# Half of the layer norm with features on the partitions, in a fused attention and MLP kernel on one core

## The chip, the core and the metric

One core of a Trainium2 chip runs the program. The core has five engines with a queue each: PE (matmuls; its weight loads are listed as PEld), DVE, ACT and POOL (elementwise work), and SP, which here issues most transfers. An engine takes its instructions in the order in which the program lists them. Transfers are carried out by 16 DMA engines. The metric is the device time of one execution in microseconds (us), median over runs; less is better.

## The reference

```python
xn = (x - mean(x)) / sqrt(var(x) + 1e-5)              # x: 2048 tokens x 512 features
q, k, v = split(xn @ wqkv)                            # 32 heads of 16 features
s = softmax(q @ k.T / 4) @ v @ wo
h = relu(xn @ w1 + b1) ** 2                           # 1792 hidden features
out = x + s * silu(h @ w2 + b2)
```

Everything is float32. The kernel gets that accuracy from faster matmuls by splitting an operand into a high part (rounded) and a low part (the rest), and adding three products: high x high, high x low, low x high.

## The kernel before

The 2048 tokens are handled as 16 tiles of 128 (t = 0 to 15) and as four chunks of 512 (c = 0 to 3). All matmuls on the normalised input need it with features on the partitions: `xTs[c]` holds chunk c as [128 partitions, high/low, 4 feature blocks, 512 tokens].

**Lead-in, up to the first side round.** For each tile: `load_x` loads 128 tokens on the partitions; `ln_stats` takes mean and variance on DVE (L1369, L1371) and the root of the variance on ACT (L1373); `ln_norm` forms scale and offset on DVE (L1378, L1379) and applies them (DVE L1383 for tiles 0 and 1, ACT L1387 behind that); `ln_high` transposes the tile with four matmuls against the identity (PE L1394) and copies the high part out of PSUM (ACT L1396); `ln_low` subtracts to get the low part (DVE L1402). The weights for the first projections come as `wm` (query and key columns of the first eight heads) and `wv` (value columns), and are split by ACT and POOL (`split_w`, L1136, L1137, L116, L117).

Projections of a finished chunk are PE work in tiles of 12 matmuls, 512 columns wide: `qk_tile(m, c)` (L1207; m = 0 to 3 are queries, 4 to 7 keys, eight heads each) and `v_tile(c, tt)` for 128 tokens (L1273). For chunk 0, queries and keys go in two halves of 256 columns. A tile occupies one PSUM bank until ACT has copied it out; queries and keys are then split by POOL, or, for the quick ones, by ACT and DVE (L122, L123), and stored to the memory tensors `q_d` and `k_d` (L1162); values go through one of seven buffers `vt` to `v_d` (L1285). PE's list is mixed by the loop over i, which pumps some matmuls of the oldest open tile behind each tile's transposes.

Before the first side round PE has done 16 tiles: keys m = 4 of all four chunks, queries m = 0 of chunks 0 to 2, values of chunks 0 and 1 and the first of chunk 2. The keys of the first four heads are read back into `ka` (12 loads, L181) and the queries into `qm` (L170). Part of `xTs` is also written out for the MLP (`spill`, L1458, and two copies into a free `ka` buffer, L1538).

**Side rounds.** From L1303 on, PE does the other projections in halves of 64 partitions, two at a time, mixed with the score matmuls from which DVE takes the row maxima (L401, L408). The rest of the kernel (exponentials, products with the values, the MLP, the output projection) follows; its order comes from planned tables. The change leaves all of that as it is.

**What sets the order.** In the lead-in the orders of PE, DVE, ACT and POOL are those in which the code is written. SP's order is set by the framework's scheduler until the side rounds begin, and by the code from there on. Transfers use eight semaphores in turn, so that a transfer is issued only when the one eight places before it has landed.

Of the kernel before, what the change touches and what calls it, by code (L numbers as in the profile page):

```python
# [9 lines left out]
F32 = mybir.dt.float32  # L10
# [63 lines left out]
def kernel(  # L74
    ctx: ExitStack,
    tc: tile.TileContext,
    x: bass.AP,
    wqkv: bass.AP,
# [18 lines left out]
    sp_d = dram.tile([S, D], F32, name="sp_d")  # L97
    xn_d = dram.tile([2, P, KO, S], F32, name="xn_d")
# [33 lines left out]
    with ExitStack() as ph:  # L132
# [42 lines left out]
        def load_k(qd, n):  # L175

            p, j, i = n // 6, n // 3 % 2, n % 3
            if n % 6 == 0:
                kas[qd, p] = ring("ka")
            h = 4 * qd + 2 * p + j  # L180
            nc.sync.dma_start(  # L181
                kas[qd, p][64 * j + DH * i : 64 * j + DH * (i + 1), :].bitcast(F32),
                k_d[h // 8][i % 2, (h % 8) * DH : (h % 8 + 1) * DH, :],
            )
# [13 lines left out]

        def load_q(u, name):
            tiles = []  # L200
            for p in range(2):
                load_q_pair(u, name, p, tiles)
            return tiles
# [928 lines left out]
        def split_w(dst, kos, cols, raw, pool=False):  # L1132
            if pool:
                split((dst[:, 0, kos, cols], dst[:, 1, kos, cols]), raw)
                return
            nc.scalar.activation(dst[:, 0, kos, cols], raw, AF.Copy)  # L1136
            nc.gpsimd.tensor_tensor(  # L1137
                dst[:, 1, kos, cols], raw, dst[:, 0, kos, cols].bitcast(F32), op=ALU.subtract
            )

        def load_w(name, width, at, kos=(KO,)):
            raw = st.tile([P, KO, width], F32, name=name)
            k0 = 0
            for n in kos:
                nc.sync.dma_start(
                    raw[:, k0 : k0 + n],
                    wqkv[:, at + k0 * width : at + (k0 + n) * width].rearrange(
                        "p (k n) -> p k n", n=width
                    ),
                )  # L1150
                k0 += n
            return raw
# [28 lines left out]
        held = []  # L1181
        hold = [True]

        def when_done(fn):
            if hold[0]:
                held.append(fn)
            else:
                fn()

        def let_go():  # L1190
            while held:
                held.pop(0)()

# [8 lines left out]
        def qk_tile(m, c):  # L1202
# [750 lines left out]
```

## Time and profile before

| | |
|---|---|
| median of 3 runs | 1571.35 us (1570.82 to 1571.38) |
| profiled execution | 1571.16 us, of which the span of instructions is 1569.3 |
| transfers, 0 to 20 us | 83% of the 16 DMA engines busy, 291 GB/s |
| 20 to 40 us | 96%, 305 GB/s |
| 40 to 60 us | 91%, 218 GB/s |
| PE's first transposes | at 6.21 us |
| PE's first side round | at 62.36 us |

The views are read so. The page gives busy time and share of each engine, and the chain of work that ended last. A list of waits names, for an engine, whose end ended its idle time: total, count, longest. A timeline has start, length, engine, line, operation, operands and shape, count, and in brackets the idle time before. A row of windows has the stretch, its length, then busy time and instructions of PE, PEld, DVE, ACT and POOL, PE's granted clock, the share of the DMA engines that was busy, and GB/s. Groups (by line and shape) have count, total busy time, mean ns of one, and idle time before them.

### The profile page before, as it was taken

The page shows a single profiled execution, that of the slowest core. Times are in us where ns is not written, and L with a number is a line of the kernel's source. Part 1 is how long each engine was busy: PE and PEld are TensorE (multiplying, and loading weights), DVE is VectorE, ACT ScalarE, POOL GpSimd, SP SyncE. Part 2 cuts the span into 40 slices and gives each one's busy share as a digit, 9 for nine tenths or more (in the row PEclk, how much of TensorE's full clock was granted, in tenths as well). Part 3 has the DMA queues.
Part 4 walks back from the last instruction along what each step waited for, and adds up shares of the span by engine and source line. Part 5 has one row for each costly group of instructions (what it writes and reads, how often), then busy time and mean ns, then how long its engine had stood idle before and what let it go on. Part 6 is the DMA issues. An engine that isn't in the chain of part 4 may idle for free.

```text
span 1569.3 us, 34206 instructions
## 1 busy us (share of the span) xinstructions
PE 1557.0 (99%) x12364; PEld 872.9 (56%) x12364; DVE 1342.3 (86%) x2307; ACT 1279.3 (82%) x2507; POOL 805.9 (51%) x824
## 2 busy tenths in 40 slices
PE   8999999999999999999999999999999999999998
PEld 7899755555555555555555555555555555555553
DVE  7377899999989998999899999998999999887765
ACT  7222788888889888888898888888888888888886
POOL 6346787348645543354465434545654345654621
PEclk9999999999999999999999999999999999999999
DMA  8967666224544531345244322533552143347665
GB/s 296 255 237 233 198 200 183 51 58 129 173 111 137 148 88 38 77 142 129 73 137 139 71 56 72 157 103 81 145 150 57 37 107 90 75 119 220 205 203 179
DMA packets 152216, 210.11 MB, mean 134 GB/s; under 512 B 58192, under 2 KB 71248, under 8 KB 150480
## 3 DMA queue, kind: packets, MB, share of 16 engines
q1 hardware_dynamic: 151904, 207.67, 46.5%
q8 instruction: 98, 1.61, 0.4%
q14 instruction: 70, 0.57, 0.1%
q10 hardware_dynamic: 144, 0.26, 0.0%
HBM read 141.56 MB, written 63.68 MB: 131 GB/s over the span
## 4 chain that ended last, share of the span: by engine, by line
PE 98%; DVE 1%; DMA 1%; issue 0%; ACT 0%; SPq 0%; DVEq 0%
PE se L487 17%; PE se L1434 12%; PE po L487 9%; PE pd_t L275 8%; PE pm_t L275 8%; PE pm_t L401 7%; PE pm_t L1434 7%; PE se L401 5%; PE pm_t L487 5%; PE pm_t L1303 4%; PE po L1434 4%; PE pd_t L401 2%; PE pm_t L243 2%; PE po L401 1%; PE pd_t L1303 1%; PE se L1273 1%
## 5 line engine op out<-in xcount | busy, mean ns | idle before, releaser
L408 DVE TENSOR_REDUCE mx<-pm_t 128x1 f32<-128x512 f32 x898 | 590.2, 682 | 50.3 <-PE pm_t L401 36.7
L1446 ACT ACTIVATE pt<-se 128x512 f32<-128x512 f32 x983 | 570.5, 623 | 30.4 <-PE pm_t L275 10.2
L408 DVE TENSOR_REDUCE mx<-se 128x1 f32<-128x512 f32 x716 | 478.3, 684 | 90.5 <-PE se L401 62.5
L1434 PE MATMUL se<-qe,ka 64*128 64x512 f32 x1086 | 434.4, 414 | 0.0
L401 PE MATMUL pm_t<-ka,qm 64*128 64x512 f32 x898 | 347.8, 398 | 0.0
L1446 ACT ACTIVATE pt<-pm_t 128x512 f32<-128x512 f32 x546 | 326.9, 622 | 8.9 <-PE pm_t L275 3.9
L1434 PEld LDWEIGHTS se<-qe,ka 64*128 64x128 f32 x1086 | 195.6, 184 | 201.6 <-ACT pt L1446 129.6
L487 PE MATMUL se<-pt,v 128*32 128x512 f32 x2224 | 282.1, 602 | 0.0
L401 PE MATMUL se<-ka,qm 64*128 64x512 f32 x716 | 281.8, 412 | 0.0
L1683 POOL TENSOR_TENSOR sum<-sum,sum 128x512 f32<-128x512 f32 x99 | 127.8, 1291 | 186.3 <-ACT sum L1682 185.9
L1683 POOL TENSOR_TENSOR ot<-ot,sum 128x512 f32<-128x512 f32 x99 | 127.7, 1290 | 180.2 <-ACT sum L1682 180.0
L1434 PE MATMUL pm_t<-qe,ka 64*128 64x512 f32 x575 | 219.0, 407 | 0.0
L275 PE MATMUL pm_t<-w2t,hT 64*128 64x512 f32 x780 | 206.6, 398 | 0.0
L1446 ACT ACTIVATE pt<-po 128x512 f32<-128x512 f32 x299 | 186.7, 625 | 7.8 <-PE pm_t L275 3.8
L401 PEld LDWEIGHTS pm_t<-ka,qm 64*128 64x128 f32 x898 | 164.0, 184 | 35.6 <-DVE mx L408 4.0
L275 PE MATMUL pm_t<-xc,w1s 64*128 64x512 f32 x672 | 177.3, 396 | 0.0
L275 PE MATMUL pd_t<-xc,w1s 64*128 64x512 f32 (+1 forms) x672 | 170.9, 388 | 0.0
L408 DVE TENSOR_REDUCE mx<-pd_t 128x1 f32<-128x512 f32 x233 | 158.7, 681 | 1.5 <-PE pd_t L401 1.5
L408 DVE TENSOR_REDUCE mx<-po 128x1 f32<-128x512 f32 x201 | 137.4, 683 | 22.2 <-PE po L401 18.7
L275 PE MATMUL pd_t<-w2t,hT 64*128 64x512 f32 x564 | 149.3, 397 | 0.0
L401 PEld LDWEIGHTS se<-ka,qm 64*128 64x128 f32 x716 | 131.4, 184 | 21.0 <-DVE mx L408 7.9
L275 PEld LDWEIGHTS pm_t<-w2t,hT 64*128 64x128 f32 x780 | 139.5, 184 | 4.4
(225 smaller groups left out, 2956.9 us busy)
## 6 DMA issues: line engine op xcount, KB each, us to landing
w1s<-w_d SPq DMA_DIRECT2D x84, 256.0 KB
w2t<-w_d SPq DMA_DIRECT2D x42, 512.0 KB
qm<-q_d SPq DMA_DIRECT2D x384, 32.0 KB
ka<-k_d SPq DMA_DIRECT2D x96, 128.0 KB
qe<-q_d SPq DMA_DIRECT2D x384, 32.0 KB
q_d<-hl SPq DMA_DIRECT2D x16, 512.0 KB
g<-g_d SPq DMA_DIRECT2D x32, 256.0 KB
k_d<-hl SPq DMA_DIRECT2D x15, 512.0 KB
```

The lines of the kernel that those rows point to most:

```text
L243: mm = nc.tensor.matmul(out_() if callable(out_) else out_, lh(r), rh(r), start=first_ and lane == 0, stop=last_ and lane == 1, skip_group ...
L275: mm = nc.tensor.matmul(out_() if callable(out_) else out_, lh(r), rh(r), start=first_ and lane == 0, stop=last_ and lane == 1, skip_group ...
L401: nc.tensor.matmul(ps, qms[u][p][64 * j : 64 * j + 64, qb * P : (qb + 1) * P], kas[qd, p][64 * j : 64 * j + 64, kc * 512 : (kc + 1) * 512] ...
L408: return nc.vector.tensor_reduce(mxs[u][:, c, kc : kc + 1], ps, axis=AX.X, op=ALU.max)
L487: nc.tensor.matmul(po[32 * j : 32 * j + 32, :], vs[qd][:, (4 * kb + j) * VW : (4 * kb + j) * VW + 32], pts[j], start=first, stop=last, ski ...
L1273: nc.tensor.matmul(out_, lh(slice(0, P)), rh(slice(0, P)), start=first_, stop=last_)
L1303: mm = nc.tensor.matmul(out_, lh(r), rh(r), start=first_ and lane == first, stop=last_ and lane != first, skip_group_check=True,)
L1434: nc.tensor.matmul(se, kas[qd, j // 2][b : b + 64, kb * P : (kb + 1) * P], qes[u][j // 2][b : b + 64, :], start=True, stop=True,)
L1446: return nc.scalar.activation(pts[j], se, AF.Exp, scale=0.25)
L1683: nc.gpsimd.tensor_tensor(pos["sum"], pos["sum"], part, op=ALU.add)
```

## The change

Tiles 0 to 7 are handled as before, except that PE's transposes are a step of their own (`ln_turn`). For chunks 2 and 3 the host lays out a second input, the same x with features on the partitions: `A_x_columns`, four groups (g = 2 to 5) of 256 tokens. For each group the tokens are also loaded with tokens on the partitions, two to a partition (`load_rows`), only to take mean and variance (`row_stats`). For a chunk, the moments of its 512 tokens, [128, 2 groups, mean or 1/deviation, 2], are written to memory (`row_out`) and read back to every partition (`row_in`, 512 KB), both from ACT's queue. DVE then subtracts the mean and multiplies by 1/deviation on the columns (`column_norm`, two operations on 128 x 1024), ACT copies the high part (`column_high`), DVE forms the low part (`column_low`). There are no transposes for these eight tiles. Column group 2 is loaded into the buffer of `wm`; groups 3, 4 and 5 share two buffers.

The lead-in is a written list of steps instead of a loop, with SP's transfers in it. Three other things move in it: the value weights are split by ACT and POOL as the other weights are; the first keys are read back in pieces, chunks 0 and 1 together (12 loads of half the old size), chunk 2 alone (12 of a quarter), and chunk 3 directly from the buffer in SBUF (12 moves), some of them from ACT's queue; the spills and copies for the MLP and the two bias loads stand behind the keys.

```diff
+        def row_stats(g, j):
+            c, h = divmod(g + 2, 2)
+            if h == j == 0:
+                moments[c] = xp.tile([P, 2, 2, 2], F32, name="mvg", bufs=2)
+            stats = xp.tile([P, 6], F32, name="stats")
+            nc.vector.bn_stats(stats, rows[g][:, j])
+            nc.vector.bn_aggr(moments[c][:, h, :, j], stats)
...
+        def row_out(c):
+            nc.scalar.dma_start(st_d[c], moments[c])
+
+        def row_in(c):
+            spread[c] = xp.tile([P, P, 2, 2, 2], F32, name="sb", bufs=2)
+            nc.scalar.dma_start(
+                spread[c].rearrange("p a h s j -> p (a h s j)"),
+                st_d[c].rearrange("a h s j -> (a h s j)")[None, :].to_broadcast([P, 1024]),
+            )
+
+        def column_norm(g, i):
+            c, h = divmod(g + 2, 2)
+            v = columns[g].rearrange("p k (a j) -> p k a j", j=2)
+            nc.vector.tensor_tensor(
+                v, v, spread[c][:, None, :, h, i, :].to_broadcast([P, KO, P, 2]),
+                op=(ALU.subtract, ALU.mult)[i],
+            )
+
+        def column_high(g):
+            c, h = divmod(g + 2, 2)
+            nc.scalar.activation(
+                xTs[c][:, 0, :, h * 256 : (h + 1) * 256], columns[g], AF.Copy
+            )
+
+        def column_low(g, eng):
+            c, h = divmod(g + 2, 2)
+            sl = slice(h * 256, (h + 1) * 256)
+            eng.tensor_tensor(
+                xTs[c][:, 1, :, sl], columns[g], xTs[c][:, 0, :, sl].bitcast(F32),
+                op=ALU.subtract,
+            )
...
-        for i in range(NT + 3):
...
+        ln_scale(3)
+        ln_root(4)
+        ln_turn(2)
+        ln_norm(3)
...
+        ln_turn(3)
+        ln_stats(6)
+        ln_norm(4)
+        matmuls(("qk", 0, 0), 12)
...
+        load_columns(5)
...
+        move_k(5, nc.scalar)
+        fill_ring("qe", 0, 0.0)
+        load_k(0, 1, 2, 3, nc.sync)
+        load_k(0, 3, 2, 3, nc.scalar)
...
+        "A_x_columns": _np.asarray(inputs["A_x"])
+        .reshape(S, D)[1024:]
+        .reshape(4, 256, KO, P)
+        .transpose(0, 3, 2, 1),
```

Rows of the built programs show the three places that matter for PE. The first is the start of PE's list, before the change (`pm_t` are transposes, `se` the first projections of chunk 0, 256 columns wide, from `xT_193`):

```order
L1394 MATMUL pm_t<-ident,xn 128x128 x8
L1207 MATMUL se<-xT_193,wa_t 128x256 x10
L1394 MATMUL pm_t<-ident,xn 128x128 x4
L1207 MATMUL se<-xT_193,wa_t 128x256 x6
L1394 MATMUL pm_t<-ident,xn 128x128 x4
L1207 MATMUL se<-xT_193,wa_t 128x256 x8
L1394 MATMUL pm_t<-ident,xn 128x128 x4
```

The same place on PE after the change, where chunk 0 is `xT_195`:

```order
L1408 MATMUL pm_t<-ident,xt 128x128 x8
L1238 MATMUL se<-xT_195,wa_t 128x256 x12
L1408 MATMUL pm_t<-ident,xt 128x128 x8
L1238 MATMUL se<-xT_195,wa_t 128x256 x36
L1408 MATMUL pm_t<-ident,xt 128x128 x4
```

The transposes of tile 3 used to come behind 16 matmuls, six of them of the second projection tile, and now come behind 12, straight after those of tile 2; the other 36 matmuls of the first two projection tiles stand behind them.

The second place is the end of the normalising on DVE. Before the change (`xT_192` is chunk 3, `hl` are quick key and query splits, `mx` the first row maxima):

```order
L1402 TENSOR_TENSOR xT_192<-pm_t,xT_192 128x4x128
L1378 RECIPROCAL rstd<-rstd 128x1
L1379 TENSOR_SCALAR rstd<-mv,rstd 128x1
L1402 TENSOR_TENSOR xT_192<-pm_t,xT_192 128x4x128 x3
L123 TENSOR_TENSOR hl<-se,hl 128x512 x2
L123 TENSOR_TENSOR hl<-po,hl 128x512
L408 TENSOR_REDUCE mx<-se 128x1 x70
```

After the change (`sb` are the spread moments, `wm` and `xc` the columns, `xT_197` and `xT_194` chunks 2 and 3):

```order
L1464 TENSOR_TENSOR wm<-wm,sb 128x1024 x2
L1464 TENSOR_TENSOR xc<-xc,sb 128x1024 x2
L1478 TENSOR_TENSOR xT_197<-wm,xT_197 128x4x256
L1478 TENSOR_TENSOR xT_197<-xc,xT_197 128x4x256
L1464 TENSOR_TENSOR xc<-xc,sb 128x1024 x4
L1478 TENSOR_TENSOR xT_194<-xc,xT_194 128x4x256 x2
L1270 TENSOR_TENSOR hl<-se,hl 128x512
L405 TENSOR_REDUCE mx<-se 128x1 x70
```

The small steps per tile have become twelve wide ones in a row, and both products of the last group stand ahead of both low parts of chunk 3.

The third place is ACT around the last tiles of the list. Before the change (`vt` are copies of value tiles, `hl` of keys and queries):

```order
L122 ACTIVATE hl<-se 128x512
L1282 ACTIVATE vt_200<-se 128x32x16
L1282 ACTIVATE vt_201<-se 128x32x16
L1282 ACTIVATE vt_202<-se 128x32x16
L1282 ACTIVATE vt_196<-pd_t 128x32x16
L122 ACTIVATE hl<-po 128x512
L1282 ACTIVATE vt_197<-pd_t 128x32x16
```

After the change (`ka<-hl` are moves of chunk 3's keys, `ka<-k_d` loads of chunk 2's):

```order
L1260 ACTIVATE hl<-se 128x512
L1286 DMA ka_210<-hl 16x512 x2
L1254 ACTIVATE vt_204<-se 128x32x16
L1286 DMA ka_210<-hl 16x512
L184 DMA ka_210<-k_d_61 16x512 x3
L1286 DMA ka_211<-hl 16x512
L1254 ACTIVATE vt_198<-pd_t 128x32x16
L1286 DMA ka_211<-hl 16x512 x2
L184 DMA ka_211<-k_d_61 16x512 x2
L1264 ACTIVATE raw<-po 128x512
```

ACT now issues twelve of the key transfers, and the copies that free PSUM banks stand between them: the copy of the first tile in the bank `pd_t` comes behind three loads that need chunk 2's stored keys.

More of the change, by code (lines that the diff above doesn't have):

```diff
@@ L97 @@
     sp_d = dram.tile([S, D], F32, name="sp_d")
+    st_d = {c: dram.tile([P, 2, 2, 2], F32, name=f"st_d{c}") for c in (2, 3)}
     xn_d = dram.tile([2, P, KO, S], F32, name="xn_d")
@@ L197, in load_v @@
             vs[qd] = v
[L199 to L203, printed above, removed]
         def load_q_pair(u, name, p, tiles):
@@ L1404, in ln_low, with load_rows @@
             )
-        ahead = []
-        rest = []
-        order = []
-        def pump(n):
-            for _ in range(n):
-                while True:
-                    todo = ahead or rest
-                    if not todo:
-                        return
-                    if next(todo[0], todo) is not todo:
-                        break
-                    todo.pop(0)
+        rows, moments, columns, spread = {}, {}, {}, {}
+        def load_rows(g):
+            rows[g] = xp.tile([P, 2, D], F32, name="xg", bufs=3)
+            nc.sync.dma_start(
+                rows[g], xf[512 + g * 256 : 768 + g * 256, :].rearrange("(p j) d -> p j d", j=2)
+            )
@@ new lines, in row_root, with row_scale @@
+        def row_root(c):
+            m = moments[c][:, :, 1]
+            nc.scalar.activation(m, m, AF.Sqrt, bias=eps_t)
+        def row_scale(c):
+            m = moments[c][:, :, 1]
+            nc.vector.reciprocal(m, m)
+        def row_out(c):
[5 more added lines that the diff above has]
+                st_d[c].rearrange("a h s j -> (a h s j)")[None, :].to_broadcast([P, 1024]),
+            )
@@ new lines @@
+        ln_scale(5)
+        ln_root(6)
+        low_w(wa_t, slice(3, 4), slice(2 * P, 2 * P + D), raw_v)
+        ln_scale(6)
+        ln_norm(5)
+        row_stats(2, 0)
+        matmuls(("qk", 4, 0), 6)
+        ln_norm(6)
+        matmuls(("qk", 4, 0), 6)
+        fill_ring("qm", 0, 0.0)
+        row_stats(3, 0)
+        matmuls(("qk", 0, 0), 12)
+        copy_out(("qk", 4, 0))
+        ln_stats(7)
+        fill_ring("qm", 1, 0.0)
+        row_stats(2, 1)
+        ln_root(7)
+        ln_turn(4)
@@ new lines @@
+        split_out(("qk", 4, 0))
+        copy_out(("qk", 0, 0))
+        matmuls(("v", 0, 0), 3)
+        ln_scale(7)
+        load_rows(5)
+        ln_high(4)
+        row_stats(3, 1)
+        matmuls(("v", 0, 0), 3)
+        ln_norm(7)
+        ln_low(4)
+        matmuls(("v", 0, 0), 3)
+        row_root(2)
+        split_out(("qk", 0, 0))
+        store(("qk", 4, 0))
+        row_scale(2)
+        row_stats(4, 0)
+        row_out(2)
+        matmuls(("v", 0, 0), 3)
+        ln_turn(5)
+        row_stats(4, 1)
@@ L1564 @@
-        rest.clear()
-        order += [("qk", m, c) for c in range(4) for m in (1, 5, 2, 6, 3, 7)]
-        specs = order[at:]
+        matmuls(("qk", 4, 3), 12)
+        load_k(0, 6, 0, 2)
+        high_w(wr_t, slice(2, 3), slice(0, 3 * P), raw_r)
+        split_out(("qk", 4, 2))
+        high_w(wr_t, slice(3, 4), slice(0, 3 * P), raw_r)
+        load_k(0, 7, 0, 2)
+        load_k(0, 8, 0, 2)
+        load_k(0, 9, 0, 2)
+        load_k(0, 10, 0, 2)
+        low_w(wr_t, slice(1, 2), slice(0, 3 * P), raw_r)
```

497 lines of the change are left out of this document (318 added, 179 removed).

## The prediction

> **What bounds the kernel now.** I read the page first (busy shares, chain that ended last), then the waits of PE over the whole run, then PE's timeline over the first 64 us.
>
> ```profile
> PE 1557.0 (99%) x12364; PEld 872.9 (56%) x12364; DVE 1342.3 (86%) x2307; ACT 1279.3 (82%) x2507; POOL 805.9 (51%) x824
> PE 98%; DVE 1%; DMA 1%; issue 0%; ACT 0%; SPq 0%; DVEq 0%
> PE pm_t L1394 <- DVE rstd L1378: 6.2, 1, 6.2
> PE se L1207 <- ACT xT L1396: 0.8, 1, 0.8
> PE po L487 <- DVE tsm L992: 0.2, 1, 0.2
> ```
>
> The first two rows are the page's: PE holds 98% of the chain that ended last. The other three are all the waits of PE in the run: 7.0 us before the first 9 us are over, and 0.2 us after. So the kernel ends when PE has worked off its list, and the change is worth what it takes off that list or adds to it as waits. The next rows are PE's timeline (start, length, line, operands, count; a merged length runs to the last one's drained end, so I use differences of starts).
>
> ```profile
> 6.21 1.94 PE L1394 MATMUL pm_t<-ident,xn 128*128 128x128 f32 x8 [6.21 <-DVE rstd L1378]
> 8.98 2.60 PE L1207 MATMUL se<-xT,wa_t 128*128 128x256 f32 x10 [0.84 <-ACT xT L1396]
> 11.38 1.05 PE L1394 MATMUL pm_t<-ident,xn 128*128 128x128 f32 x4
> 12.08 1.05 PE L1207 MATMUL se<-xT,wa_t 128*128 128x256 f32 x6
> 13.17 0.66 PE L1394 MATMUL pm_t<-ident,xn 128*128 128x128 f32 x4
> 16.79 1.91 PE L1207 MATMUL se<-xT,wa_t 128*128 128x256 f32 x14
> 18.54 0.60 PE L1394 MATMUL pm_t<-ident,xn 128*128 128x128 f32 x4
> 19.21 2.48 PE L1273 MATMUL se<-wa_t,xT 128*128 128x512 f32 x10
> 37.00 3.03 PE L1273 MATMUL se<-wa_t,xT 128*128 128x512 f32 x12
> 39.87 5.76 PE L1207 MATMUL se<-xT,wa_t 128*128 128x512 f32 x24
> 62.36 0.50 PE L1303 MATMUL pm_t<-wa_t,xT 64*128 64x512 f32 x1
> ```
>
> At 62.36 the first side round (L1303) starts. From there on the order of every engine is the same in both programs, and PE waits for 0.2 us in all, so the whole effect is the shift of this one start, unless new waits appear behind it. I call it S: 62.36 before.
>
> **Term 1, the transposes that go.** From 39.87 to 62.36 stand eight tiles of 12 matmuls: 22.49 / 96 = 0.234 us each, 2.81 a tile. From 19.21 to 37.00 stand 60 such matmuls and nine groups of four transposes: (17.79 - 60 x 0.234) / 9 = 0.41 us a group, what it costs its neighbours included. Eight groups of sixteen go: 3.3 us.
>
> **Term 2, the start.** PE now does transposes of tiles 2 and 3 ahead of the second projection tile, so it stands at tile 3's transposes until tile 3 is normalised. That is late, since DVE and ACT do the moments and the root of tile 4 before tile 3's scale and norm, and tile 4 is now the ninth transfer, behind both value-weight loads.
>
> ```profile
> 10.87 0.33 SPq L1361 DMA_DIRECT2D xt<-in_A_x_dram  x1
> 12.13 1.01 SPq L1361 DMA_DIRECT2D xt<-in_A_x_dram  x2
> SPq L1361 <- DMA wv<-in_A_wqkv_dram: 1.8, 2, 0.9
> 11.10 0.66 DVE L1369 BATCH_NORM_STATS2 stats<-xt 128x6 f32<-128x512 f32 x1
> 12.01 0.29 ACT L1373 ACTIVATE rstd<-mv,eps_t 128x1 f32<-128x1 f32 x1 [0.50 <-DVE rstd L1378]
> 12.30 0.81 ACT L1387 ACTIVATE xn<-xt,rstd 128x512 f32<-128x512 f32 x1
> ```
>
> SP's queue rows show two loads of x issued at 10.87 and 12.13, each when one half of the value weights had landed (the third row: SP waited for wv). In bytes, tile 4 now lies halfway between those two, so it lands at about 11.45. The chain from there is in the old rows: moments at 11.10, root at 12.01, norm at 12.30, transposes at 13.17, 2.07 us in all. The new transposes of tile 3 start at 11.45 + 2.07 = 13.52, against 13.17. Behind them stand 36 matmuls of 256 columns ((18.54 - 16.79) / 14 = 0.125 each; 0.119 without the first one of the group, which I use), five transpose groups and fourteen tiles: 13.52 + 5 x 0.41 + 36 x 0.119 + 14 x 2.81 = 59.2. So without any wait S moves from 62.36 to 59.2, a gain of 3.1: the 3.3 of term 1, and 0.2 lost at the start.
>
> **Term 3, the columns.** Rows of x for the second half are loaded twice, once for moments, once as columns; moments go out to memory and come back on every partition. DVE does four row moments and one tile's between its third low part and the reciprocal (0.86 us each by the rows below), so ACT issues the moments at about 21.7.
>
> ```profile
> L1369 DVE BATCH_NORM_STATS2 stats<-xt 128x6 f32<-128x512 f32 x16 | 10.9, 683 | 2.1 <-DMA xt<-in_A_x_dram 2.1
> L1371 DVE BATCH_NORM_AGGREGATE mv<-stats 128x2 f32<-128x6 f32 x16 | 2.9, 182 | 0.6
> L1402 DVE TENSOR_TENSOR xT<-pm_t,xT 128x512 fp32r<-128x512 f32 x16 | 11.0, 686 | 5.5 <-ACT xT L1396 5.3
> L993 DVE TENSOR_TENSOR rb<-rb,tsm 128x256 f32<-128x256 f32 x2 | 0.9, 426 | 0.1
> L1136 ACT ACTIVATE wa_t<-wm 128x512 fp32r<-128x512 f32 x2 | 1.2, 625 | 0.0
> L1136 ACT ACTIVATE wr_t<-wv 128x384 fp32r<-128x384 f32 x4 | 1.8, 515 | 0.0
> 317.91 0.34 SPq L461 DMA_DIRECT2D sh_d<-sh  x1
> 319.40 2.10 SPq L478 DMA_DIRECT2D qe<-sh_d  x4
> 191.31 0.46 SPq L461 DMA_DIRECT2D sh_d<-sh  x1
> 195.50 2.19 SPq L478 DMA_DIRECT2D qe<-sh_d  x4
> 0.74 2.67 DMA xt<-in_A_x_dram
> ```
>
> The small write sh_d and the read that waits for it bound the round trip: 1.5 us on an idle queue, 4.2 on a busy one; I take 2.3, near the idle end, because ACT's queue holds nothing else. A load of 256 KB took 2.67 us; 512 KB is 0.65 more (the step between two x loads, half of 12.13 - 10.87), 3.3, and 1.3 for sharing with the column loads. The spread moments are there at about 29 (28 to 31 by these bounds). A DVE operation of 512 takes 0.69 and of 256 0.43, so one of 1024 takes 1.2; ACT, 0.52 for 384 and 0.63 for 512, takes 1.0. PE now works from a list that I can date: the first value tile starts at 18.6, the key tile of chunk 1 ends at 33.9, the value tile v(1,1) at 42.3, key chunk 3 starts at 45.1. DVE's four products for columns 2 and 3 end at 33.6, just ahead of ACT's turn for their high part (34.7, behind the copy of the key tile). Its low part ends at 36.8, only then may column group 5 load (two buffers), which lands at 40.1; two products to 42.4, two low parts, and the last one, which also waits for ACT's high part of 44.0, ends at 45.2. Key chunk 3 needs it from its second matmul, at 45.3. This cover is 0.1 us, so I count a loss of 0 to 0.5 here. Chunk 2, by the same chain, is ready at 36.8 for 42.3.
>
> **Term 4, the keys.** Quarter-width key loads and SBUF moves now stand on ACT's queue too, with PSUM copies between them.
>
> ```profile
> 50.81 6.46 SPq L181 DMA_DIRECT2D ka<-k_d  x12
> L117 POOL TENSOR_TENSOR hl<-raw,hl 128x512 fp32r<-128x512 f32 x4 | 5.2, 1292 | 0.3
> 67.97 1.15 SPq L1145 DMA_DIRECT2D wv<-in_A_wqkv_dram  x1
> 77.53 1.75 ACT L1136 ACTIVATE wr_t<-wv 128x384 fp32r<-128x384 f32 x4
> 58.00:60.00 2.00, 2.00 (x10) 1.60 (x10) 0.00 (x0) 0.29 (x1) 0.00 (x0) 1.00 1.06 131
> ```
>
> The twelve old loads ran at 131 GB/s (last row, last column), 1.0 us for each 128 KB. The halves that replace them are issued once chunk 1's keys have landed, but lie behind 768 KB of weights and two stores until about 45.5, and take 0.5 us each: to 51. Chunk 2's keys are written behind them, landing at about 53; ACT's third load waits for that, and the copy of v(1,3) stands behind it and three more, at about 55.9. The last value tile of the list needs that copy's bank at 56.4. If the writes are 1 us later, PE waits 0.5. POOL splits these weights and chunk 2's keys (1.3 us a low part) by 51, wanted at S: nothing, with 8 us of cover. Spills, the copies of xT and the bias loads are moved behind the keys, ahead of the second part of these weights: about 7 MB from 56 on, so that part lands at about 76 instead of the 75 or so behind its issue at 67.97. ACT, which used it at 77.53, now comes 3 us earlier and waits about 1.5; the bank whose copy stands behind that is wanted four tiles later, so I count nothing.
>
> For terms 3 and 4 together I take 0.4 us, the middle of 0 to 0.8. **The sum:** -3.1 + 0.4 = -2.7. The profiled execution took 1571.16 (span 1569.3, so 1.9 around it), giving 1568.5; the median of the runs, 1571.35, is 0.2 higher: 1568.6. A measurement tells about 0.2%, 3.14 us, from no change, so the limit is 1568.2.
>
> **Rivals.** *No new wait, and a better start* (0.25): if tile 4 lands 0.5 us earlier, or the 0.58 us that PE loses between 13.17 and 19.21 (6.04, against 4 x 0.41 + 32 x 0.119 = 5.45) hid other costs, the gain is 3.2 to 4.3: 1567.1 to 1568.1. For it: the tight places are tight only by my dates.
>
> *The first rounds stay at half rate longer* (0.07). The first eight transposes stand at 6.21 with 1.94 for all, 0.21 each when the tail is left out; later four take 0.35 from 18.54 to the next matmul. So PE starts at half speed, and the group at 11.38, 0.70 long up to 12.08, still has most of it. The new list leaves PE idle for some 0.5 us ahead of 13.5. [...]
>
> *Slower: the spread moments are read slowly* (0.11). The products read pairs of values that lie 32 bytes apart; no row has that. Below, nothing makes them faster than the 1.2 of plain rows; above, if one takes e us more, columns 3 are late by 4e - 1.1 and group 5 by 2e more, so PE waits at key chunk 3 for 6e - 1.2. At e = 1.2 (half rate) that is 6.0, and the kernel ends 2.9 above the old time, at 1574.2; from e = 1.25 it is measurably slower. [...] I keep 1.2, since the row with tsm, which repeats one value, is as fast as plain ones, but it does not settle this.
>
> *The key writes are late* (0.12): 1 to 3 us more on the queue ahead of chunk 2's keys holds ACT, the bank and PE by 0.5 to 2.5: 1569.1 to 1571.1.
>
> **How the numbers follow.** The forecast itself has 0.45: 1567.9 to 1569.2, of which 0.10 lies below 1568.2. Faster: 0.10 + 0.25 = 0.35. Slower: 0.08 of the 0.11, since moments that come late add to the same wait. Same: the rest, 0.57. The range leaves out the slow products above and the best starts below, 2 in 10 at most: 1567.0 to 1571.6.
>
> **What would show it.** Transposes of tile 3 at 13.5 in PE's timeline; S at 59.2 to 59.7; no wait of PE between 14 and 45, one of at most 0.5 at key chunk 3 on DVE's low part, one of at most 0.5 at v(2,0) on ACT. Products of 1.2 us. It is wrong if S lies before 58.8 or after 60.2, or if PE waits behind S.

## The result, and the profile after

The changed kernel takes **1589.61 us** (median of 4 runs, 1586.09 to 1591.53) against 1571.3 in the same job: a ratio of 1.0115, 95% interval 1.0094 to 1.0135. It is slower, where 1568.6 was forecast, and lies far outside the range given. The profiled execution took 1586.09, its span 1584.3: 15.0 us more than the span before. It is the fastest of the four, and the account below is of these 15.0 us. One profiled execution, that of e11, ran at a mean clock of 0.87 and is not read.

The page of the changed kernel first, busy times and the chain that ended last:

```profile
PE 1561.0 (99%) x12332; PEld 866.4 (55%) x12332; DVE 1350.1 (85%) x2295; ACT 1276.4 (81%) x2493; POOL 810.7 (51%) x824
PE 94%; DMA 2%; DVE 2%; SPq 1%; ACT 0%; issue 0%; DVEq 0%; ACTq 0%
```

PE has its 32 transposes less (12332 against 12364), yet its share of the chain fell from 98% to 94%: something else stands in it. The largest waits of PE, as before total, count and longest:

```profile
PE pm_t L1408 <- DVE xt L1398: 8.3, 2, 6.2
PE pd_t L1238 <- ACT vt L1254: 3.0, 1, 3.0
PE se L1238 <- ACT xT L1471: 2.8, 1, 2.8
PE pm_t L1314 <- ACT raw L1188: 2.8, 1, 2.8
```

Three smaller rows, not shown, hold 1.4 us. Before, three rows held 7.2 us. Now there are 2 us more at the start and three new waits of about 3 us, the first of them in two parts (2.8 and 0.5). PE's timeline (start, length, line, operands, count, idle time before) says where:

```profile
9.35 1.11 PE L1408 MATMUL pm_t<-ident,xt 128*128 128x128 f32 x4 [2.07 <-DVE xt L1398]
11.15 2.93 PE L1238 MATMUL se<-xT,wa_t 128*128 128x256 f32 x12 [0.69 <-ACT xT L1412]
49.55 0.80 PE L1238 MATMUL se<-xT,wa_t 128*128 128x512 f32 x1 [2.77 <-ACT xT L1471]
50.81 5.06 PE L1238 MATMUL se<-xT,wa_t 128*128 128x512 f32 x11 [0.47 <-DVE xT L1478]
55.67 3.13 PE L1238 MATMUL se<-wa_t,xT 128*128 128x512 f32 x12
67.35 5.49 PE L1238 MATMUL pd_t<-wa_t,xT 128*128 128x512 f32 x12 [2.96 <-ACT vt L1254]
72.77 0.66 PE L1314 MATMUL pm_t<-wa_t,xT 64*128 64x512 f32 x1
98.64 1.65 PE L1314 MATMUL pm_t<-wa_t,xT 64*128 64x512 f32 x12 [2.75 <-ACT raw L1188]
```

S, the start of the first side round, is 72.77, against 62.36 before and 59.2 to 59.7 forecast. The first wait is that of key chunk 3 for its columns, the second that of v(2,0) for a bank, the third that behind the second weights. Two groups are also too long. The eleven matmuls from 50.81 to 55.67 take 0.44 us each, the twelve from 67.35 to 72.77 take 0.45, where the rows before had 0.234. The windows show why (PE's busy time is the number behind the length; the granted clock stands ahead of the last two):

```profile
45.83:49.24 3.41, 0.95 (x5) 0.44 (x3) 3.29 (x3) 2.06 (x3) 0.00 (x0) 1.00 1.03 361
49.24:52.66 3.42, 2.64 (x5) 1.78 (x6) 1.52 (x2) 2.51 (x6) 1.59 (x2) 0.50 0.85 311
52.66:56.07 3.41, 3.41 (x9) 2.65 (x8) 0.00 (x0) 0.16 (x1) 3.39 (x4) 0.50 0.24 63
56.07:59.48 3.41, 3.41 (x16) 2.77 (x15) 0.69 (x1) 1.04 (x2) 3.20 (x6) 1.00 0.09 19
```

The clock is recorded as full from 15.11, half from 49.24, full from 56.07, half from 66.31 and full from 73.14: 10, 2, 3 and 2 times 3.41 us. In the 3.41 us ahead of 49.24 PE had been busy for 0.95. It then ran at half clock for two such stretches, and again from 66.31 to 73.14. So each of the first two waits of 3 us cost nearly 6. The third did not: it lay across two stretches, with PE busy for 2.27 and 1.80 us of 3.41, and the clock stayed full.

The 10.4 us that S is late add up so: the forecast without waits, 3.1 early; the start, where the first value tile stands at 20.14 in place of 18.6, 1.5 late; the waits ahead of S, 2.77 + 0.47 + 2.96 = 6.2; half clock, 11 x (0.442 - 0.234) + 12 x (0.452 - 0.234) = 4.9, and 0.6 for the one matmul at 49.55. Together 10.1, so 0.3 stay open. Behind S come 2.75 for the third wait; the last 1.9 of the 15.0 gather in small steps over 1,480 us, and what they are stays open too.

Why the columns were late, from DVE's and POOL's timelines of the changed kernel:

```profile
33.02 2.50 DVE L1464 TENSOR_TENSOR wm<-wm,sb 128x1024 f32<-128x1024 f32 x2 [3.19 <-DMA sb<-st_d]
37.84 1.64 DVE L1478 TENSOR_TENSOR xT<-wm,xT 128x1024 fp32r<-128x1024 f32 x1
39.40 2.31 DVE L1478 TENSOR_TENSOR xT<-xc,xT 128x1024 fp32r<-128x1024 f32 x1
41.63 3.88 DVE L1464 TENSOR_TENSOR xc<-xc,sb 128x1024 f32<-128x1024 f32 x2
48.32 2.44 DVE L1478 TENSOR_TENSOR xT<-xc,xT 128x1024 fp32r<-128x1024 f32 x2
```

```profile
37.26 1.15 POOL L118 TENSOR_SCALAR hl<-raw 128x512 fp32r<-128x512 f32 x1 [8.40 <-ACT raw L1264]
38.49 2.13 POOL L119 TENSOR_TENSOR hl<-raw,hl 128x512 fp32r<-128x512 f32 x1
40.60 1.59 POOL L118 TENSOR_SCALAR hl<-raw 128x512 fp32r<-128x512 f32 x1
42.27 2.15 POOL L119 TENSOR_TENSOR hl<-raw,hl 128x512 fp32r<-128x512 f32 x1
```

DVE's products start at 33.0, not 29. Alone they take 1.25 each, 2.50 for two. Beside POOL's splits of chunk 1's keys and queries an operation of DVE takes 1.6 to 2.3, and POOL's 1.29 becomes 2.1. The ends alternate: POOL 38.41, DVE 39.48, POOL 40.62, DVE 41.71. Each ends some 1.1 us after the other, about what it takes alone: they take turns.

Why the bank was late, from the waits between 45 and 100 us on ACT, then on SP:

```profile
ACT vt L1254 <- DMA ka<-k_d: 7.3, 1, 7.3
```

```profile
SPq L184 <- DMA ka<-hl: 4.9, 1, 4.9
SPq L1158 <- DMA ka<-hl: 1.5, 1, 1.5
```

```profile
56.54 1.30 ACTq L1286 DMA_DIRECT2D ka<-hl  x2
61.76 0.38 SPq L1158 DMA_DIRECT2D k_d<-hl  x1
64.83 1.27 ACTq L184 DMA_DIRECT2D ka<-k_d  x3
```

SP stood 4.9 us, at a load of chunk 1's keys, for a move (`ka<-hl`) that ACT issues. They share no data: the load uses the same one of the eight semaphores. The move left ACT at 56.54, landed at 58.51, and the load was issued at 58.53. Chunk 2's key store (L1158) came behind it, at 61.76, after 1.5 us for the semaphore of another such move. ACT's next load waited for that store, with the copy of v(1,3) queued behind. The move itself could leave only when chunk 3's keys were split, at 56.52, and the first wait had put these back: so the late columns are in the second wait too.

### The profile page after: what moved, and what is told of

Same layout as the page of the kernel before. It is cut to its first block, busy times and chain, and to the rows that moved or that the text cites. A ratio compares the mean times of both kernels' runs of the same rounds, so it can differ in the third digit from the quotient of the medians.

```text
span 1584.3 us, 34141 instructions
## 1 busy us (share of the span) xinstructions
PE 1561.0 (99%) x12332; PEld 866.4 (55%) x12332; DVE 1350.1 (85%) x2295; ACT 1276.4 (81%) x2493; POOL 810.7 (51%) x824
## 4 chain that ended last, share of the span: by engine, by line
PE 94%; DMA 2%; DVE 2%; SPq 1%; ACT 0%; issue 0%; DVEq 0%; ACTq 0%
PE se L484 17%; PE se L1497 12%; PE po L484 9%; PE pm_t L272 8%; PE pd_t L272 8%; PE pm_t L1497 7%; PE pm_t L398 6%; PE se L398 5%; PE pm_t L484 5%; PE po L1497 4%; PE pm_t L1314 3%; PE pd_t L398 2%; PE pm_t L240 2%; PE po L398 1%; PE pd_t L240 1%; PE pd_t L1314 1%
## 5 line engine op out<-in xcount | busy, mean ns | idle before, releaser
L1509 ACT ACTIVATE pt<-se 128x512 f32<-128x512 f32 x983 | 571.6, 625 | 30.0 <-PE pm_t L272 10.1
L398 PE MATMUL se<-ka,qm 64*128 64x512 f32 x716 | 271.7, 411 | 0.0
L1497 PEld LDWEIGHTS pm_t<-qe,ka 64*128 64x128 f32 x575 | 103.1, 184 | 68.7 <-ACT pt L1509 44.4
```

The lines of the kernel that those rows point to most:

```text
L398: nc.tensor.matmul(ps, qms[u][p][64 * j : 64 * j + 64, qb * P : (qb + 1) * P], kas[qd, p][64 * j : 64 * j + 64, kc * 512 : (kc + 1) * 512] ...
L1497: nc.tensor.matmul(se, kas[qd, j // 2][b : b + 64, kb * P : (kb + 1) * P], qes[u][j // 2][b : b + 64, :], start=True, stop=True,)
L1509: return nc.scalar.activation(pts[j], se, AF.Exp, scale=0.25)
```

## The experiments

The order is that of the runs. Ratios are to the kernel before in the same job, whose median lay between 1570.76 and 1571.63. S and the waits are those of one profiled execution each, and S scatters: up to there e3 issues the same work as the change, and has S 4.1 us earlier, with a start 1.5 earlier and one stretch at half clock instead of four.

| kernel | median us | ratio, 95% | S | waits of PE behind 14 us that matter |
|---|---|---|---|---|
| the change | 1589.61 | 1.0115 (1.0094, 1.0135) | 72.8 | columns 3.2, bank 3.0, weights 2.8 |
| e1, keys on SP | 1586.96 | 1.0096 (1.0079, 1.0113) | 67.6 | columns 4.1, weights 8.7 |
| e2, column buffer | 1587.12 | 1.0101 (1.0086, 1.0116) | 72.6 | columns 3.3, bank 3.1, weights 2.6 |
| e3, weights first | 1578.75 | 1.0047 (1.0032, 1.0062) | 68.7 | columns 5.1, bank 2.1 |
| e4, busy PE | 1586.07 | 1.0093 (1.0078, 1.0108) | 66.9 | columns 0.6, weights 4.9 |
| e5, e1 and e3 | 1577.61 | 1.0035 (1.0023, 1.0047) | 67.4 | columns 3.2 |
| e6, e5, value tile ahead | 1576.50 | 1.0030 (1.0018, 1.0041) | 63.6 | columns 1.7, keys 1.1, late stores 1.3 |
| e7, e5, columns early | 1574.73 | 1.0019 (1.0010, 1.0028) | 65.1 | columns 2.5 |
| e8, all of these | 1573.27 | 1.0010 (1.0001, 1.0019) | 59.6 | keys 1.5, late stores 1.9 |
| e9, e8, moves on ACT | 1576.71 | 1.0038 (1.0024, 1.0052) | 60.7 | columns 0.8, keys 4.8 |
| e10, e9, early spills | 1577.58 | 1.0043 (1.0030, 1.0057) | 59.4 | keys 5.6 |
| e11, e8, early spills | 1575.83 | 1.0029 (1.0018, 1.0040) | | |
| e12, e11, keys by memory | 1574.30 | 1.0020 (1.0011, 1.0030) | 60.1 | keys 4.3 |
| e13, e12, stores first | 1575.27 | 1.0024 (1.0015, 1.0033) | 60.4 | keys 3.8 |
| e14, e13, spills late | 1569.79 | 0.9992 (0.9983, 1.0002) | 62.0 | none |
| e15, e14, start filled | 1569.54 | 0.9990 (0.9981, 0.9999) | 59.4 | none |
| e16, e15, root back | 1569.74 | 0.9990 (0.9981, 0.9999) | 60.8 | none |

### One place at a time, and the clock

**e1**: all twelve key transfers of chunks 2 and 3 that were ACT's go to SP.

```diff
-        move_k(3, nc.scalar)
+        move_k(3, nc.sync)
...
-            load_k(0, 3, 2, 3, nc.scalar)
+            load_k(0, 3, 2, 3, nc.sync)
```

> The changed kernel with all 24 key transfers of chunks 2 and 3 issued by SP; nothing is left out. Theory A (the copy of v(1,3) stands on ACT behind loads that wait for chunk 2's stored keys, and SP itself waited 4.9 us at L184 for a move that ACT issued): PE's wait of 3.0 at the tile v(2,0) falls below 0.5 and the half rate behind it goes, so about 3 + 2.7 less: 1583 to 1585 against 1589.6. Theory B (the keys are late whoever issues them): the wait moves to the first row maxima, PE waits there for 2 to 4 us, and the time stays within 1.5 of 1589.6.

**e2**: a buffer of its own for column group 5, in the rows' pool, and its load early.

```diff
+            elif g == 5:
+                columns[g] = xp.tile([P, 2, D], F32, name="xg", bufs=3).rearrange(
+                    "p j (a n) -> p (j a) n", n=256
+                )
...
         store(("v", 0, 1))
+        load_columns(5)
```

> The changed kernel with column group 5 in a third buffer (one of the row buffers, free by then), loaded right behind the store of v(0,1); nothing is left out. Theory A (group 5's load, 41.7 to 45.9, stood behind chunk 2's last low part): DVE goes on from group 4 to group 5 without a gap, its last low part ends 2 to 3 us earlier, PE's waits of 2.8 + 0.5 at key chunk 3 fall to about 1, and the half rate behind them goes if the wait is short: 1585 to 1587. Theory B (the late spread moments, there at 32.9, and DVE beside POOL set it): the wait stays above 2 and the time within 1.5 of 1589.6.

**e3**: the second weights are loaded ahead of the spills, the biases later.

```diff
         store(("v", 1, 2))
+        raw_r = w_tile("wv", 3 * P)
+        load_w(raw_r, KO * (5 * P + D), 0, KO)
         spill(0, 0)
```

> The changed kernel with the second part of the later weights loaded ahead of the spills, and the two bias loads put behind the ninth group of row maxima; nothing is left out. Theory A (ACT's copy of the query tile of chunk 3 stood behind the split of these weights, which landed at 96.3): PE's wait of 2.8 at 98.6 goes, 2.8 to 3.1 less: about 1586.6. Theory B (that wait is made up later, since the engines behind run ahead): no change beyond 1 us.

**e4**: twelve extra matmuls, whose result is overwritten, ahead of key chunk 3 and again ahead of v(2,0).

```diff
+        idle_work(pd.tile([P, 512], F32, name="pd_t"), 12)
         matmuls(("qk", 4, 3), 12)
```

> The changed kernel with 12 matmuls of no use (2.8 us at full rate, results dropped) ahead of key chunk 3 and 12 more ahead of the tile v(2,0), where PE waited 3.2 and 3.0 us. Theory A (half of what the waits cost is the half rate that follows them, 6.8 us each by the granted clock): the waits are filled, the granted clock stays at 1.0 between 49 and 73 us, the starts of matmuls behind stay 0.23 apart, and the time falls by 4 to 5.5: 1584 to 1586. Theory B (the matmuls behind the waits are slow for another reason, such as their operands): they stay 0.43 apart and the time is the same or up to 5.6 more.

PE's largest waits in e1:

```profile
PE pm_t L1314 <- ACT raw L1188: 8.7, 1, 8.7
PE pm_t L1408 <- DVE xt L1398: 8.0, 2, 6.2
PE se L1238 <- ACT xT L1471: 3.6, 1, 3.6
```

The bank's wait is gone, as theory A has it, and S comes 5 us earlier; but the second weights still land at about 96 us, since their place on SP's queue sets that, and PE waits there for what S gained. So the time missed its 1583 to 1585. e4 tells the same: its extra work took the place of both waits, the clock held up to the weights, S came 6 us earlier, and 4.9 us and a stretch at half clock were lost near 94 us. It also shows the cause of the slow matmuls, in the eleven that had taken 0.44 each behind the wait for columns:

```profile
50.20 2.83 PE L1238 MATMUL se<-xT,wa_t 128*128 128x512 f32 x11 [0.57 <-DVE xT L1484]
```

They now take 0.24. Only e3, which moves the weights, lets a gain reach the end: 10.9 us, where 3 were forecast. In the profiles it is 7.0, of which 4.1 lie ahead of S, where this edit changes nothing. The clean pair is e1 and e5 below: S is 67.6 and 67.4, e3's edit is all that differs, and the time falls by 9.4. So the weights' place was a floor under everything ahead. e2 left the wait for columns as it was (3.3 for 3.2): the load of group 5 had held DVE for 0.4 us only, and DVE's own chain sets the date. So theory B has the wait right; the time, 2.5 us lower, lies within the runs of the change.

### Several at once

**e5** is e1 with e3. **e6** is e5 with a value tile that needs no columns ahead of key chunk 3, **e7** is e5 with the first two column loads in a stretch in which the transfers had been mostly idle. **e8** has both, and two more:

```diff
         load_x(7)
+        load_columns(2)
+        load_columns(3)
...
-        matmuls(("qk", 4, 3), 12)
+        matmuls(("v", 1, 2), 12)
...
-        copy_out(("qk", 4, 1))
-        split_out(("qk", 4, 1))
+        copy_out(("qk", 4, 1), True)
+        split_out(("qk", 4, 1), True)
```

The first lines are e7's, the next pair e6's (key chunk 3 moves behind that tile). The last, also made for chunk 1's queries, have ACT and DVE split instead of ACT and POOL. Tile 1's root also goes ahead of the weights' high part.

> The changed kernel with both edits at once: all key loads and moves of chunks 2 and 3 on SP's queue, and the second weights loaded ahead of the spills. My theory: three places are late in the changed kernel, key chunk 3's columns, v(2,0)'s bank and the second weights, each draws the clock to half behind it, and what one edit saves at one place is spent at the next. With the last two gone only key chunk 3 is left: the start gives about 2 us, its wait takes 3.5 to 4.3 and half rate behind it 1 to 2.4, so S lies 4 to 5.5 us behind the kernel before and nothing is added behind S: 1575.3 to 1577.0, no wait at v(2,0) and none at L1314. Rival, that a fuller SP queue makes the second weights late again: a wait at L1314 of over 2 us, above 1579. Rival, that the drift behind S is of another origin: no wait at L1314, but still above 1580.

> The same, and on PE the tile v(1,2), which needs no columns, is put ahead of key chunk 3, its copy ahead on ACT. Theory: this gives key chunk 3's columns 2.8 us more, so of a wait of 3.5 to 4.3 and 0.5 there 1.2 to 2 are left, short enough that the clock holds; S at the old place or up to 1 us ahead: 1570.5 to 1572.0. If the clock falls after a wait of 1 to 2 us too, 2.4 more: 1573 to 1574.4. Rival, that key chunk 3's keys are now late for the maxima behind S: a new wait of 2 us or more at se<-ka,qm behind S.

> As the first of these four, but the loads of column groups 2 and 3 are issued right behind the load of tile 7, in the stretch from 19 to 23.3 us in which the DMA engines stood idle. Theory: the spread of the first moments then shares its engines with less, takes 3 to 4 us in place of 7.2, and DVE's products start at 29 to 30 in place of 32.9; the chain behind moves by the same, so key chunk 3's wait falls to 0 to 1.5: 1569.5 to 1572.5. Rival, that the spread takes 7 us by itself (a repeat of one small row on 128 partitions, whatever the load): products still at 32 to 33, and a time as in the first of the four.

> All at once: keys on SP, second weights early, v(1,2) ahead of key chunk 3, columns 2 and 3 early, and two more: the splits of chunk 1's keys and queries on ACT and DVE in place of ACT and POOL, and tile 1's root ahead of the weights' high part on ACT. Theory: low parts and products that took 1.6 to 2.3 us beside POOL's splits take 1.22 each, so DVE gives back 2.9 and pays 1.4 for the two splits; no wait of PE behind 14 us, clock full from 15 on to the end, S at 59 to 60: 1568 to 1570. Rival, that DVE's slow operations have another cause than POOL: they stay at 1.6 to 2.3.

e5 has neither the bank's wait nor that for the weights, and lies 0.6 us above its range. e6 missed by 4.5 us, and by 2.1 the range for a clock that falls: 2.4 us were waited behind S, and two short waits ahead of it still cost one stretch at half clock (windows of e6, PE busy 1.77 of 3.41 in the first):

```profile
47.97:51.38 3.41, 1.77 (x7) 0.93 (x6) 2.91 (x3) 1.69 (x3) 0.03 (x1) 1.00 0.99 382
51.38:54.79 3.41, 3.41 (x10) 2.66 (x9) 0.00 (x0) 2.12 (x5) 3.33 (x4) 0.50 0.55 146
```

In e7 the spread took 5.5 us from its issue to the first product, for 7.3 in e5. That is 1.8 us less, not the 3 to 4 that I expected; the DMA engines were still fully busy beside it (330 GB/s from 25.5 to 31.0), so what it takes by itself is not shown. The wait for columns stayed at 2.5 us, and the time came out 2 above the range. e8 settles what slowed DVE; its timeline, with POOL's split gone from it:

```profile
35.78 1.22 DVE L1478 TENSOR_TENSOR xT<-wm,xT 128x1024 fp32r<-128x1024 f32 x1
36.92 1.22 DVE L1478 TENSOR_TENSOR xT<-xc,xT 128x1024 fp32r<-128x1024 f32 x1
38.05 1.23 DVE L1464 TENSOR_TENSOR xc<-xc,sb 128x1024 f32<-128x1024 f32 x1
```

The same operations that took 1.64, 2.31 and 1.63 take 1.22. In e7, which has the early columns but keeps POOL's splits, the first two still take 1.64 and 2.31. S is 59.57, where 59.2 plus 0.4 was forecast. But the time is 1573.3, 3.3 above the range, since PE waits behind S:

```profile
PE se L398 <- DMA ka<-k_d: 1.5, 1, 1.5
PE pm_t L1314 <- ACT raw L1188: 1.2, 1, 1.2
PE pd_t L1314 <- ACT raw L1188: 0.7, 1, 0.7
```

### Behind S: SP's queue

**e9** gives six of the moves back to ACT (the first diff) and leaves the loads on SP. **e10** adds e2's buffer and early spills (the second). **e11** is e10 with all keys on SP. **e12** sends chunk 3's keys through memory again, with chunk 2's (the third).

```diff
-        move_k(3, nc.sync)
+        move_k(3, nc.scalar)
```

```diff
+        spill(0, 0)
+        spill(0, 1)
+        spill(1, 0)
         matmuls(("v", 0, 3), 12)
```

```diff
-        move_k(0, nc.sync)
-        move_k(3, nc.sync)
+        store(("qk", 4, 3))
+        load_k(0, 0, 2, 4)
+        load_k(0, 1, 2, 4)
```

> As the last kernel with all edits, but six of the twelve moves of chunk 3's keys go back to ACT's queue, and the loads that wait for chunk 2's keys stay on SP. Theory: what held ACT (7.3 us) and SP (4.9 us) in the changed kernel was not a second queue as such, but loads on ACT that wait for a write of SP; a move waits for nothing but its own split. So ACT's copies stay on time, no wait at v(2,0); SP issues six transfers of 0.5 to 0.6 us less, chunk 2's last load and all behind it come some 3 us earlier, PE's wait for ka behind S (1.5 us) shrinks to 0 to 0.8, and those at L1314 at 117 to 121 us (1.9 in all) to 0 to 1: 1570 to 1572, S unchanged at 59 to 60. Rival, that any transfers on both queues hold each other through their shared slots: ACT or SP waits of over 2 us again, and a wait of PE at v(2,0) or S later than 61.

> As the one before, and the spills of chunk 0 and of the first half of chunk 1 (2 MB) are issued at about 33 us, behind the first query loads, in place of behind the keys at 70 to 75; column group 5 in a buffer of its own, loaded ahead of them. Theory: the waits at L1314 at 117 to 121 us come from stores of keys and queries that lie on SP behind these spills (the splits on POOL wait for the stores, ACT's copies for the splits): with 2 MB, some 5 us of transfer, gone from 70 to 100 us the stores leave 3 to 5 us earlier and these waits are gone; the spread of the second moments shares with them and lands up to 3 us later, which the buffer of group 5 covers. S at 59 to 60, nothing or at most 0.5 behind it: 1568 to 1570. Rival, that the early spills make key chunk 3 late: a wait of PE at 48 us and a time as before or above. Rival, that the waits at 117 to 121 us have another cause: they stay.

> As the kernel with all edits (all keys on SP), and only the early spills and the own buffer of column group 5 of the last one. The last two showed waits at 117 to 121 us gone with the early spills, but chunk 2's keys stored at 58 in place of 52 us, with SP's loads waiting for moves on ACT. Theory: it is the moves on ACT that hold SP, through shared transfer slots; with all on SP the store leaves at 52 to 54 again, PE waits 1.5 to 2.5 for ka behind S and nothing at 117 to 121 us, S at 59 to 60: 1570 to 1571.5. Rival, that the 2 MB of spills hold the key loads: the store at 57 or later, a wait of 4 us or more for ka, 1574 or more.

> As the one before, but chunk 3's keys go through memory again: stored, and chunks 2 and 3 loaded together in twelve halves, in place of twelve moves and twelve quarters. Theory: SP issues one transfer each 0.6 us there, so 24 took from 53 to 68 us; with twelve the last is issued at 62 to 63 and what stands behind them, the second weights and the spills, leaves 5 us earlier; the first one waits for chunk 3's store and lands at 57 to 59, so PE waits for ka behind S 0 to 2 us: 1569.0 to 1571.0. Rival, that the way through memory costs more than the issues saved: ka lands later than 63 us, a wait of over 2.5 us behind S, above 1572.

All four missed their ranges. e9 goes against its theory and in part with its rival: the moves on ACT wait for nothing but their split, and still held SP, for 2.6 us at once, though v(2,0) did not wait and S stayed at 60.7. SP's eleven key loads took 10.78 us against 7.45 in e8, and chunk 2's store left at 58.3 against 52.2; of these 6.1 us, 2.2 were there before the loads began. In e10 the waits at 117 to 121 us are gone, but they are gone in e9 too, which has the spills late; so that the spills cause them is not shown. PE's wait for keys was 5.6, for 4.8, and the runs of the two overlap. The clock fell behind this wait, as behind those of e9, e12 and e13 (matmuls of 0.39 ahead take 0.62 behind it). e11 differs from e8 by the early spills and group 5's buffer alone and takes some 2.5 us more; its time is on the side of its rival, that the spills hold the key loads. So is e12 on that of its own, with 4.3 for keys. SP's timeline of e12:

```profile
44.09 0.38 SPq L1158 DMA_DIRECT2D k_d<-hl  x1
47.97 7.93 SPq L184 DMA_DIRECT2D ka<-k_d  x11
57.92 0.45 SPq L1158 DMA_DIRECT2D k_d<-hl  x1
62.10 5.40 SPq L184 DMA_DIRECT2D ka<-k_d  x12
```

The third row is chunk 3's key store. DVE had that split ready at 55.0. It stood behind eleven loads, which could not start before chunk 1's store, the first row, had landed.

**e13** moves query loads that are wanted only at S behind chunk 1's stores, and splits chunk 2's keys on ACT and DVE (the last pair); **e14** puts the spills back behind the keys.

```diff
         matmuls(("qk", 4, 2), 12)
+        load_q_pair(0, "qm", 1, qms[0])
         load_k(0, 0, 0, 2)
...
-        copy_out(("qk", 4, 2))
+        copy_out(("qk", 4, 2), True)
```

> As the kernel with the keys by memory, with SP's queue in another order: the second six query loads, wanted only at S, are issued behind chunk 1's stores, just ahead of the key loads, and chunk 2's keys are split by ACT and DVE. Theory: the last kernel's loss was all SP order, since chunk 3's store stood ready at about 53 us and left at 58 behind eleven key loads, which waited for chunk 1's stores, which lay behind query loads. Chunk 1's keys then leave at 36 to 38 in place of 44, the eleven loads end at 50 to 52, chunk 3's store leaves at 53 and the twelve loads run from 56 to 62; PE waits for ka behind S 0 to 1 us, no half rate, nothing at 117 to 121 us, S at 59 to 60: 1568.0 to 1570.0, so the gain of 3 us that was forecast for the transposes does reach the end. Rival, that the way of chunk 3's keys from PE to ka is too long whatever SP's order: a wait for ka of 3 us or more, 1572 or above.

> The same with the spills of 2 MB back behind the keys, where the change has them. Theory: the keys come as early or 1 to 2 us earlier, but the second weights and the stores at 100 to 115 us lie behind the spills again: waits of 0 to 2 us at L1314 near 117 us, 1568.5 to 1571.5. Rival, that the early spills are what held chunk 1's stores in the last kernels: then this one is the faster by 1 us or more.

The same rows of SP in e14:

```profile
38.30 0.37 SPq L1158 DMA_DIRECT2D k_d<-hl  x1
46.61 6.08 SPq L184 DMA_DIRECT2D ka<-k_d  x11
55.09 0.38 SPq L1158 DMA_DIRECT2D k_d<-hl  x1
58.35 5.41 SPq L184 DMA_DIRECT2D ka<-k_d  x12
```

Chunk 1's store leaves 5.8 us earlier and the last loads start 3.7 earlier, though PE's list stands 2 us later than in e12. PE waits for 0.2 us in all behind 15 us. e13 and e14 differ in the spills alone, by 5.5 us: with 2 MB issued at 34.6, e13's key loads start at 49.8 in place of 46.6, and its last ones at 62.0 in place of 58.4. So e13 missed; its rival, that the keys' way is too long in any order, falls with e14, and e14's rival, that the early spills held the stores, is right. So what was lost behind S was lost on SP's queue, by its order and by the moves; e14 differs from e8 in several places at once, and the share of each is not shown.

### The start

**e15** fills the wait for tile 3; **e16** undoes the root.

```diff
+        matmuls(("qk", 0, 0), 6)
         ln_turn(3)
...
-        matmuls(("qk", 0, 0), 12)
+        matmuls(("qk", 0, 0), 6)
```

> As the last kernel (spills late), with six of the twelve matmuls of the first query tile put ahead of tile 3's transposes on PE, which need only tiles 0 and 1. Theory: with no wait left behind 14 us, only the start decides. The last profile waited 0.8 us for tile 3's norm at 14 us, full clock came at 19.1 us in place of 12 to 15 in the other kernels, and S lay at 62.0. With the gap filled (6 matmuls are 0.7 us at full rate, 1.4 at half) there is no wait at tile 3, full clock at 13 to 15 us, S at 59 to 60.5: 1567.0 to 1569.2, less scatter between runs than the 4 us of the last one. Rival, that the late clock comes from the earlier gap, 1.4 us ahead of the first product: full clock still at 19 in some runs and a scatter as before.

> As e15_start_filled, with tile 1's root back behind the high part of the first weights on ACT, where the change has it. Theory: this gap moves only from before the first product (1.4 us) to before tile 1's transposes (0.2 to 2.1 us, by when the first weights land): within 1 us of the kernel beside it, 1567 to 1570. Rival, that the root ahead was what held the first product and so the clock: faster by over 1 us.

e14 lies within its range, e15 0.3 us above its own, and e16 within. In the profile of e14 full clock came at 19.1 us, in that of e15 at 13.0, with S at 59.41:

```profile
13.91 0.60 PE L1408 MATMUL pm_t<-ident,xt 128*128 128x128 f32 x4
59.41 0.50 PE L1314 MATMUL pm_t<-wa_t,xT 64*128 64x512 f32 x1
```

The profiled execution of e15 took 1568.66, its median is 1569.54 (11 runs, 1568.66 to 1571.96): the interval of its ratio, 0.9981 to 0.9999, lies just below 1. e15 and e16 can't be told apart, and the runs of e15 still scatter over 3.3 us, so which gap of the start matters more stays open. These two are the versions that beat both kernels, the one before by 1.5 to 1.7 us, a tenth of a per cent.

## Why the prediction was wrong

**Term 1, the transposes: right.** With every wait behind 16 us gone but 0.2, S lies at 59.41 in e15, for 59.2 without waits by the sum, and from the first value tile to S it takes 40.57 us, for 40.6 by the sum. The gain of 3.0 in S appears as 2.4 in the span (1569.3 to 1566.9); that execution is the fastest of its eleven, and the median gains 1.7.

**Term 2, the start: mis-sized by 1.5 us, by two things.** The value tile forecast at 18.6 stood at 20.14. Tile 3's transposes started at 14.7, for 13.52 forecast, but PE did not wait for them: from 11.15 on it had no gap, at half clock. What was late was tile 1's norm on DVE. Its root stood on ACT behind the first weights' high part (at 7.51, for 5.21 before), and the norm took 1.02 beside POOL, for 0.55. So the first product stood at 11.15 for 8.98 before, and its twelve matmuls took 0.23 each, where the 36 from 15.28 on took 0.125; the record of the clock begins, with full, at 15.11 for 12.31. The rival "the first rounds stay at half rate longer", at 0.07, is what came; what sets the moment of full clock is not shown. The runs show a late one in most kernels here: in ten of the fifteen experiments' profiles full clock came behind 13.5 us, against 12.31 before.

**Term 3, the columns: this step failed.** "So I count a loss of 0 to 0.5 here" measured 3.2 us of wait and 2.9 of half clock. Three numbers failed in it. The moments came at 33.0, outside the bounds of 28 to 31: the write was issued at 23.1 for 21.7, it took 2.5 us, and the read 7.4, beside row, key, column and query transfers, where 3.3 + 1.3 was allowed. DVE's operations were taken at 1.2; four of them ran beside POOL and took 7.8 in place of 4.9. And no cover was left, as the text itself said (0.1 us). Group 5's load, on which the text spent most care, was worth 0.4.

The rows for the 1.2 could not show that price. The low part of before reads one input from PSUM and took 0.69 beside POOL, for a mean of 0.686, while the operation on `tsm`, with both in SBUF, has a second row in the same view (its two operations took 0.42, and 0.65 for the one that began with one of POOL's):

```profile
13.63 0.69 DVE L1402 TENSOR_TENSOR xT<-pm_t,xT 128x512 fp32r<-128x512 f32 x1 [0.25 <-ACT xT L1396]
13.74 1.29 POOL L117 TENSOR_TENSOR wa_t<-wv,wa_t 128x512 fp32r<-128x512 f32 x1
L993 DVE TENSOR_TENSOR tt<-tt,tsm 128x256 f32<-128x256 f32 x2 | 1.1, 539 | 0.1
```

With two inputs in SBUF the trace of the change shows the price in the alternating ends above (1.64 and 2.31 for a low part), and e8 shows 1.22 without it. The prediction weighed a slow read of the spread moments instead. That rival fell: they are read at 1.25 us an operation.

**Term 4, the keys: this step failed too, with the right mechanism.** The text named the chain (chunk 2's write, ACT's load behind it, the copy of v(1,3), its bank) and dated that copy 55.9; it came at 66.70. "Landing at about 53" was 64.8. What it lacked is the semaphores, which its own account of the kernel names: moves on ACT held SP for 4.9 and 1.5 us, and through them the late keys of chunk 3 held those of chunk 2, so that terms 3 and 4 were not apart. The loads had also begun 2.7 late, at 48.16 for 45.5; the rest of the 12 us is in shorter waits on SP and a write of 3 us for 2. The rival "the key writes are late" allowed 1 to 3 us; it was 12. e1 shows the share: with the keys on one queue, S is 5 us earlier.

**The second weights: "I count nothing" was worth 2.8 us, and more as a floor.** They landed at 96 us, not 76. The 7 MB ahead of them were counted, but from 56; the keys held their start on SP's queue to 72.07, and the weights were issued at 89.99. From e1 to e5, with S equal, e3's edit is worth 9.4 us.

**Not in the sum at all: the clock.** The prediction weighed it for the start only. Each of two waits of 3 us cost another 2.6 to 2.9 us behind it. PE was not idle for all of the 3.41 us ahead: it was busy for 0.95 of them ahead of the first fall, and for 1.50, from 62.89, ahead of the second.

## What to carry to other kernels

Where one engine holds 98% of the chain, taking work off it pays only if every feeder keeps its lead: date each feeder against the new list, price it beside what runs next to it (DVE's 1.22 became 1.6 to 2.3 beside POOL) and what shares its queue or semaphore (SP stood 4.9 us for a move of ACT), and count a wait of 3 us on PE as up to double, for the clock (2.6 to 2.9 us more here). Mending the first late place shows little while a later one has a fixed date (e1, e4), so look for the last such date first (e3). What is wanted late must not stand ahead, on a queue, of what is waited for (e14).

## What the runs showed of the hardware that was not expected

- The clock fell behind stretches in which PE was partly busy. Behind those of 3.41 us with PE busy for 0.95 and 1.50 (the change) and 1.77 us (e6) the next ran at half clock; behind the one in e8 with its wait of 1.5 us it did not (row below). The busy time alone does not set it: in e3 a stretch with 1.66 us busy, from 43.74, was followed by full clock (its matmul at 49.68 took 0.50, where that at 49.55 in the change, at half clock, took 0.80). At half clock, stretches with 2.64 us (the change) and 2.93 (e5) busy did not bring full speed back; one with 2.92 (e13) and one with 3.04 (e3) did. What decides stays open.

```profile
61.18:64.59 3.41, 1.92 (x15) 1.03 (x11) 1.45 (x3) 0.59 (x2) 3.20 (x4) 1.00 0.24 55
```

- DVE's operations with two float32 inputs in SBUF and POOL's splits took turns, operation by operation, their ends some 1.1 us apart: on 128 x 1024 DVE took 1.22 to 1.25 us alone, 1.6 to 2.3 beside POOL, and POOL's 1.29 on 128 x 512 became 2.15. DVE's subtraction with one input in PSUM took 0.69 beside POOL, for a mean of 0.686 over all sixteen.
- Pairs of float32 that lie 32 bytes apart were read about as fast as plain rows: 1.25 us for 128 x 1024, where the low part, on plain rows, took 1.22 (e8).
